# Block combination and transposition moved by one step, and the first gates made on TensorE, in a state-space and expert-mixture kernel

## The chip, the cores and the metric

The kernel runs on one core of a Trainium2 chip. The metric is the device time of one execution in microseconds (us); the median of several executions is compared. A core has these engines, each with its own queue of instructions that runs in order: PE (TensorE, matrix products into PSUM), DVE (VectorE), ACT (ScalarE), POOL (GpSimd) and SP (SyncE, which here issues most transfers). Everything is in float32.

## The reference

A Mamba-2 state-space block (4 sequences, 8 heads, 768 positions, head width 32, state 16) feeds a merge of four expert networks. Cut to what matters:

```python
# block 1, by chunks of the sequence, state carried along
cum = np.cumsum(log_a[chunk]);  L = exp(cum_i - cum_j) * causal
y = (C @ B.T * L) @ x + (C @ state) * exp(cum)
state = exp(cum_last) * state + sum_j B_j x_j exp(cum_last - cum_j)
# block 2, on rows of 256 = 8 heads * 32
p = domain_probs / (domain_probs.sum(-1, keepdims=True) + 1e-09)
for e in range(4):
    h = np.maximum(x @ w1[e], 0.0)            # 256 -> 1024
    out += p[:, e:e + 1] * (h @ w2[e])        # 1024 -> 256
```

## The kernel before, in words

**Tiling.** The sequences are cut into 24 chunks of 128 tokens. A block is four chunks, the same place of all four sequences: 512 tokens, and there are six blocks (k = 0 to 5). For every block the expert part takes eight steps (r = 0 to 7; an expert e is two steps, each with half of its hidden width), 48 steps in all (n = 8k + r). The state-space part of the next block's chunks is woven into the steps of the current block: chunk c comes in (`masks`, `decay_part`, `scores`, `masked`) in steps r = 0, 2, 4, 6, and goes out (`outputs`, later `carry`) in steps r = 1, 3, 5, 7. In the last block no chunk comes in.

**A step.** From step 2 on both layers are done by a fast scheme of seven products for a 2x2 split of the matrices instead of eight. `fmul(n, i)` is product i of the first layer (L436, four pieces on PE, into the PSUM banks X and Y); `snap` copies X on ACT (L443); `total` adds Y and a copy to z on DVE (L448); `gated` applies the ReLU and the gate on DVE (L458); `diff` makes the differences T1 to T4 that the second layer needs (L465, DVE). `smul(n - 1, i)` is product i of the second layer of the step before (L521), into four PSUM accumulators `acc0` to `acc3`, each held for a whole block. The first two steps use the eight plain products (`plain_first` L485, `plain_second` L502). `sum_w1` and `sum_w2` make sums of weights on POOL (L160 to L164) in the first block and store them in DRAM for the later ones (`w1_d`, `w2_d`).

**Order.** The schedule is written out by hand: every engine runs its instructions in the order of the program text, and the framework adds the waits. A tile with a tag shares a fixed number of buffers; taking one anew waits for all readers of the old one. Two waits of this kind matter here: a new product into Y waits for the `total` that read it, and the first `smul` of a block into an accumulator waits for the readers of the block before. Transfers use eight counters in turn, so that a transfer also waits for the eighth before it.

**The end of a block.** In step r = 0 of block k the last products of block k - 1 are made. `keep` copies `acc0` and `acc1` to SBUF (ACT). `combine(k - 1, 0)` adds on DVE into u (L541), `combine(k - 1, 1)` makes four adds on POOL (L544 to L547), both at the end of step r = 0. `combine(k - 1, 2)`, two adds on DVE from `acc2` and `acc3` (L549, L550; a third, L552, in the first block), is in the list `late`, which runs in step r = 1 behind `gated(n, "11")`, after the differences T2 and T4. Then `turned_out` transposes 32x32 squares on DVE (L610), and `leave` sends the rows to the output with eight transfers on SP's queue (L618), one quarter of the block in each of the steps r = 1 to 4.

**The first gates.** The normalized probabilities `pr` are transposed by PE (L266), copied by ACT to `p_sb`, 96 rows of 128 (L268), and stored by ACT's queue in DRAM as `p_d` (L269). `load_gate(k, e)` then reads the rows of a block and an expert and spreads each over all 128 partitions (L273, SP's queue, 256 KB). Before step 2, the front of the program, the order on DVE is: `masked(2)` (L363), `decays(3)` (L330, two scans), `plain_gated(0, 1)` (two `gated`, the first readers of a gate), `masked(3)`, `plain_gated(1, 1)`; on PE: `outputs(1)` (L382), `scores(2)` (L353), `plain_first(0, 1)`, `outputs(2)`, `scores(3)`, `plain_first(1, 1)`, `outputs(3)`, `plain_second(0, 1, ...)`. `outputs(c)` waits for `masked(c)`.

Of the kernel before, what the change touches and what calls it, by code (L numbers as in the profile page):

```python
# [17 lines left out]
def kernel(  # L18
# [90 lines left out]
    def load_decays(c, queue):  # L109
        if c >= SPREAD:  # L110
            ab = load.tile([P, NH * P], FP32, tag="ab", name="ab")
            nc.sync.dma_start(
                out=ab, in_=acut_d[real(c)].rearrange(
                    "h s -> (h s)").partition_broadcast(P))
            st.setdefault(c, {})["ab"] = ab
        if c >= CPB:
            ah = st[c]["ah"] = load.tile([HN, P], FP32, tag="ah", name="ah")
            queue.dma_start(out=ah, in_=ac_d[real(c)].unsqueeze(1).to_broadcast([NH, N, P]))
# [19 lines left out]
    def load_w2(n):  # L138
        e, jj = divmod(n % SPB, JJ)
        t2 = wt2[n] = wts.tile([P, 7 * HB], FP32, tag="wt2", name="wt2", bufs=5)  # L140
        if n >= SPB:
            nc.sync.dma_start(out=t2, in_=w2_d[n % SPB])
            return
        for i in range(2):
            f = i * FH + jj * HB
            nc.sync.dma_start(
                out=t2[:, i * 2 * HB:(i + 1) * 2 * HB].rearrange("p (j m) -> p j m", j=JJ),
                in_=w2[e, f:f + HB].rearrange("(j p) m -> p j m", p=P))
# [113 lines left out]
    def turn_gates():  # L262

        rows = T // P * E
        pp = ps_att.tile([rows, P], FP32, tag="att", name="pp")
        nc.tensor.transpose(pp, pr.rearrange("p i e -> p (i e)"), ident[:, 0])  # L266
        p_sb = const.tile([rows, P], FP32, name="p_sb")
        nc.scalar.copy(out=p_sb, in_=pp)  # L268
        nc.scalar.dma_start(out=p_d.rearrange("i e s -> (i e) s"), in_=p_sb)  # L269

    def load_gate(k, e):
        g = gate[k, e] = ffn.tile([P, CPB, P], FP32, tag="gate", name="gate", bufs=3)
        nc.sync.dma_start(out=g, in_=p_d.rearrange(  # L273
            "(i k) e s -> k e i s", k=NBLK)[k, e].partition_broadcast(P))
# [71 lines left out]
    def scores(c, homes):  # L346

        s = st[c]
        s["g"] = []
        for q, (pool, tag) in enumerate(homes):  # L350
            k = slice(32 * q, 32 * q + 32)
            g = pool.tile([P, NT, P], FP32, tag=tag, name="g")
            nc.tensor.matmul(  # L353
                out=g.rearrange("p t s -> p (t s)"), lhsT=s["xb"][k, OBT:OBT + P],
                rhs=s["ctm"][k].rearrange("p t s -> p (t s)"),
                start=True, stop=True, tile_position=(32 * q, 0))
            s["g"].append(g)
# [9 lines left out]
    def outputs(c, pool, tag):  # L367

        s = st[c]
        k, i = divmod(c, CPB)  # L370
        first = k == 0
        w = P + N if k < NBLK - 1 else P
        xb, MT = s["xb"], s["MT"]
        y = pool.tile([P, NT, P + N], FP32, tag=tag, name="y")
        if not first:
            nc.tensor.matmul(  # L376
                out=y[:, :, 0:P], lhsT=state[i][1].rearrange("p q d -> p (q d)"),
                rhs=s["cts"], start=True, stop=False, skip_group_check=True)
        for t in range(NT):
            for q in range(NQ):  # L380
                h = NQ * t + q
                nc.tensor.matmul(  # L382
                    out=y[32 * q:32 * q + 32, t, 0:w], lhsT=xb[:, h * D:h * D + D],
                    rhs=MT[:, NT * q + t, 0:w], start=(first and t == 0), stop=True,
                    tile_position=(0, 32 * q), skip_group_check=True)
        if i == 0:
            yT[k] = ffn.tile([P, NT, BLK], FP32, tag="yT", name="yT")
        nc.scalar.copy(out=yT[k][:, :, i * P:i * P + P], in_=y[:, :, 0:P])
        if w > P:
            s["A"] = att.tile([P, NT, N], FP32, tag="A", name="A", bufs=4)  # L390
            nc.scalar.copy(out=s["A"], in_=y[:, :, P:])
# [83 lines left out]
    def plain_first(n, b, a=(0, 1)):  # L475

        k = n // SPB
        cols = slice(b * HB - HB, b * HB)
        f = first.setdefault(n, {})
        for bank, ws in [(("X", (A11, A12)), ("Y", (S3, A22)))[i] for i in a]:  # L480
            pool, tag = (ps_f, bank) if n or b > 1 else (ps_s, {"X": "acc2", "Y": "acc3"}[bank])
            f[bank] = pool.tile([P, JJ, HB], FP32, tag=tag, name=bank)
            for j in range(JJ):
                for i, w in enumerate(ws):
                    nc.tensor.matmul(  # L485
                        out=f[bank][:, j], lhsT=wt1[n][:, w, j * P:j * P + P],
                        rhs=yT[k][:, i, cols], start=(i == 0 and j == 0), stop=(i == 1),
                        skip_group_check=True)
# [171 lines left out]
    sum_w1(0, 0)  # L660
    masked(1, range(NQ))
    outputs(1, ps_att, "att")
    load_decays(3, nc.sync)
    load_w2(1)
    load_w1(2)
    load_w2(2)

    scores(2, homes)
    plain_first(0, 1)
    decays(2)  # L670
    sum_w1(1, 0)
    masks(3)
    load_gate(0, 0)
    load_chunk(4)
    load_gate(0, 1)
    load_w1(3)
    load_w2(3)
    masked(2, range(NQ))
    outputs(2, ps_att, "att")

# [3 lines left out]
    load_w1(4)  # L684
    load_w2(4)
    sum_w2(0, 0)
    plain_gated(0, 1)
    plain_first(1, 1)
    masked(3, range(NQ))
    sum_w2(1, 0)  # L690
# [28 lines left out]
    for n in range(PLAIN, NS):  # L719
        k, r = divmod(n, SPB)  # L720

        enter, exit = ({2: 1, 4: 2, 6: 3}, {2: 0, 3: 1, 5: 2, 7: 3}) if k == 0 else (
            {0: 0, 2: 1, 4: 2, 6: 3}, {1: 0, 3: 1, 5: 2, 7: 3})
        c_in, c_out = (CPB * (k + 1) + d[r] if r in d and k < NBLK - 1 else None
                       for d in (enter, exit))
        ending = r == 0 and k > 0
        e = r // JJ
        if r % JJ == 0 and n + JJ < NS:
            load_gate(*divmod(n // JJ + 1, E))
        if PLAIN + 2 < n + 2 < NS:  # L730
            load_w1(n + 2)
            load_w2(n + 2)
        opened(n)
        total(n, 1, "11")
        gated(n, "11", "z11")
        for work in late:
            work()
        if c_in is not None:
            masks(c_in)
            decay_part(c_in, 0)  # L740
        if n == PLAIN:
            for m in range(PLAIN):
                sum_w1(m, 1)
        elif n == PLAIN + 1:
            for m in range(1, PLAIN):
                sum_w2(m, 1)
        sum_w1(n + 2)
        if n > PLAIN:
            sum_w2(n + 1)
        if r == 1 and k > 0:  # L750
            turned_out(k - 1)
        if k > 0 and 1 <= r <= CPB:
            leave(k - 1, r - 1)
        smul(n - 1, 1)
        fmul(n, 6)
        snap(n, 6)
        smul(n - 1, 3)
        if ending:
            keep(k - 1, 0)
        if c_out is not None:  # L760
            outputs(c_out, ps_att, "att")
        fmul(n, 5)
        fmul(n, 7)
        snap(n, 7)
        total(n, 7, "22")
        smul(n - 1, 7)
        smul(n - 1, 5)
        if ending:
            keep(k - 1, 1)
        gated(n, "22", "z22")  # L770
        if c_in is not None:
            decay_part(c_in, 1)
        if n == PLAIN:
            sum_w2(0, 1)
        if c_out is not None and c_out + 2 < NCH:
            load_chunk(c_out + 2)
        fmul(n, 3)
        total(n, 6, "12")
        fmul(n, 4)
        gated(n, "21", "X")  # L780
        gated(n, "12", "z12")
        if r == SPB - 1 and k < NBLK - 1:
            sums(k + 1)
        smul(n - 1, 6)
        smul(n - 1, 2)
        if c_in is not None:
            scores(c_in, ((ps_att, "att"), (ps_att, "att"), (ps_f, "X"), (ps_f, "Y")))
            masked(c_in, (2, 3, 0, 1))
        diff(n, "T3", "22", "12")
        if c_in is not None:  # L790
            decay_part(c_in, 2)
        if ending:
            combine(k - 1, 0)
            combine(k - 1, 1)
        smul(n - 1, 4)
        diff(n, "T1", "12", "11")
        late = [lambda n=n: diff(n, "T2", "22", "T1"), lambda n=n: diff(n, "T4", "21", "T2")]
        if ending:
            late.append(lambda k=k: combine(k - 1, 2))
        if PLAIN < n <= CPB:  # L800
            late.append(lambda n=n: carry(n - 1))
        if c_out is not None:
            late.append(lambda c=c_out: carry(c))
# [48 lines left out]
```

## Time and profile before

| | |
|---|---|
| median of 8 runs | 662.6 us (660.0 to 663.84) |
| the profiled execution | 663.84 us; its span, first to last instruction, 662.1 us |
| mean granted clock of PE | 0.993 |
| busy share | PE 98%, DVE 74%, ACT 17%, POOL 17% |
| mean DMA rate | 192 GB/s, 127.09 MB in all |

The page gives busy times by engine, then the span in 40 slices of 16.55 us, in which a digit is a tenth of a slice, then groups of instructions by source line. `L448` is line 448 of the kernel. The list of waits has lines "who waited <- for whom: us in total, times, longest". Lines of the timeline have start and duration in us, engine (PEld is PE's loading of weights), line, operation, the tile written <- the tiles read, the shape, the number of instructions merged, and in brackets the idle time before and what ended it. A float32 product appears as two pieces on PE. The ends of pieces on PE are modelled, so lost time is read from start to start.

### The profile page before, as it was taken

The numbers are of one execution on the slowest core, as the hardware profiler recorded it, in microseconds if no ns is written. First come the engines' busy times: TensorE is split into PE (matmuls) and PEld (weight loads), VectorE is DVE, ScalarE is ACT, GpSimd is POOL, SyncE is SP. The second block draws the span as 40 slices with busy tenths as digits, with TensorE's granted clock in tenths as the row PEclk, the third lists the DMA queues.
The fourth block names the chain that finished last, engine by engine and source line by source line (L and its number), as shares of the span: only waits on it lengthen the run. The fifth ranks groups of instructions, "written<-read, shape, count | busy, mean of one in ns | idle before, by whom it ended". The sixth has DMA issues, their size and how long they took to land. (4 is left out here: it accounts for less than half of the span.)

```text
span 662.1 us, 8901 instructions
## 1 busy us (share of the span) xinstructions
PE 647.6 (98%) x3359; PEld 542.1 (82%) x3359; DVE 488.7 (74%) x814; ACT 115.1 (17%) x246; POOL 112.4 (17%) x157
## 2 busy tenths in 40 slices
PE   7899989999999999999999999999999999999997
PEld 4688868888888888888887888888888888888886
DVE  8667878798686788866879768668867686766655
ACT  3011111221112121121122111212111112111110
POOL 5757494020000002000003000000200000100000
PEclk9899989999999999999999999999999999999999
DMA  7989998404668611678630656941276751176000
GB/s 234 312 309 338 335 365 311 171 35 114 236 209 354 238 56 26 228 254 304 253 146 1 182 193 240 356 181 56 71 248 210 291 219 59 18 245 243 4 1 32
DMA packets 68666, 127.09 MB, mean 192 GB/s; under 512 B 26616, under 2 KB 50576, under 8 KB 68624
## 3 DMA queue, kind: packets, MB, share of 16 engines
q1 hardware_dynamic: 65568, 111.32, 48.7%
q0 software_dynamic: 2304, 14.68, 5.5%
q10 hardware_dynamic: 752, 0.54, 0.3%
q8 instruction: 26, 0.43, 0.2%
q14 instruction: 16, 0.13, 0.1%
HBM read 108.44 MB, written 18.07 MB: 191 GB/s over the span
## 5 line engine op out<-in xcount | busy, mean ns | idle before, releaser
L448 DVE TENSOR_TENSOR z<-Y,snap 128x512 f32<-128x512 f32 x138 | 94.5, 685 | 125.1 <-ACT snap L443 71.5
L521 PE MATMUL acc<-hT,wt 128*128 128x256 f32 x736 | 183.1, 382 | 0.0
L443 ACT COPY snap<-X 128x512 f32<-128x512 f32 x138 | 80.9, 587 | 472.5 <-PE X L436 472.5
L521 PEld LDWEIGHTS acc<-hT,wt 128*128 128x128 f32 x736 | 138.3, 190 | 24.0 <-issue 6.0
L436 PE MATMUL X<-yS,wt 128*128 128x256 f32 x552 | 141.7, 379 | 0.0
L521 PE MATMUL acc<-h,wt 128*128 128x256 f32 x552 | 141.5, 379 | 0.0
L436 PEld LDWEIGHTS X<-yS,wt 128*128 128x128 f32 x552 | 105.0, 190 | 14.4
L521 PEld LDWEIGHTS acc<-h,wt 128*128 128x128 f32 x552 | 104.9, 190 | 14.3
L458 DVE SCALAR_TENSOR_TENSOR h<-z,gate 128x512 f32<-128x512 f32 x138 | 98.7, 715 | 3.5 <-PE acc L502 0.4
L436 PE MATMUL Y<-yT,wt 128*128 128x256 f32 x368 | 94.9, 380 | 2.4 <-DVE z L448 2.4
L436 PEld LDWEIGHTS Y<-yT,wt 128*128 128x128 f32 x368 | 68.4, 189 | 14.5 <-DVE z L448 4.3
L465 DVE TENSOR_TENSOR hT<-h,hT 128x512 f32<-128x512 f32 x92 | 69.8, 759 | 1.6
L465 DVE TENSOR_TENSOR hT<-h,h 128x512 f32<-128x512 f32 x92 | 64.6, 726 | 0.8
L330 DVE TENSOR_TENSOR_SCAN LT<-ab,ident 128x512 f32<-128x512 f32 x42 | 53.5, 1276 | 0.9 <-DMA ab<-acut_d 0.9
L335 POOL TENSOR_TENSOR MT<-xb,LT 128x128 f32<-128x128 f32 x20 | 8.8, 438 | 252.0 <-PE Y L436 132.5
L436 PE MATMUL Y<-yS,wt 128*128 128x256 f32 x184 | 50.2, 396 | 0.0
L436 PE MATMUL X<-yT,wt 128*128 128x256 f32 x184 | 47.2, 379 | 0.0
L363 DVE TENSOR_TENSOR MT<-g,LT 128x256 f32<-128x256 f32 x96 | 33.9, 416 | 17.3 <-PE g L353 17.3
L316 POOL TENSOR_TENSOR cts<-ctm,dec 128x256 f32<-128x256 f32 x20 | 18.5, 927 | 160.6 <-ACT snap L443 157.7
L458 DVE SCALAR_TENSOR_TENSOR h<-X,gate 128x512 f32<-128x512 f32 x50 | 34.3, 686 | 12.1 <-PE X L436 4.6
L436 PEld LDWEIGHTS Y<-yS,wt 128*128 128x128 f32 x184 | 33.8, 192 | 8.5 <-issue 4.2
L436 PEld LDWEIGHTS X<-yT,wt 128*128 128x128 f32 x184 | 35.0, 190 | 4.8
(91 smaller groups left out, 339.2 us busy)
## 6 DMA issues: line engine op xcount, KB each, us to landing
wt<-w_d SPq DMA_DIRECT2D x80, 896.0 KB, 10.0
w_d<-wt POOLq DMA_DIRECT2D x16, 896.0 KB, 6.8
ab<-acut_d SPq DMA_DIRECT2D x21, 512.0 KB, 4.7
wt<-in_w_dram SPq DMA_DIRECT2D x32, 256.0 KB, 7.4
xb<-in_xbc_dram SPq DMA_DIRECT2D x24, 320.0 KB, 3.8
gate<-p_d SPq DMA_DIRECT2D x24, 256.0 KB, 8.7
out_dram<-ot SPq DMA_DIRECT2D x160, 16.0 KB, 5.2
ah<-ac_d SPq DMA_DIRECT2D x20, 64.0 KB
```

Source lines behind the costliest of these rows:

```text
L316: nc.gpsimd.tensor_mul(cts, s["ctm"], dec.unsqueeze(1).to_broadcast([HN, NT, P]))
L330: nc.vector.tensor_tensor_scan(out=LT[:, i * w:i * w + w], data0=s["a"][i], data1=ident.rearrange("p h s -> p (h s)")[:, :w], initial=0.0, ...
L335: nc.gpsimd.tensor_mul(s["MT"][:, :, P:], s["xb"][:, OB:OB + HN].rearrange("p (h n) -> p h n", h=NH), s["LT"][:, :, P - 1:P].to_broadcast( ...
L363: nc.vector.tensor_mul(s["MT"][:, h, 0:P], s["g"][q], s["LT"][:, h])
L436: nc.tensor.matmul(out=f[bank][:, j], lhsT=wt1[n][:, w, j * P:j * P + P], rhs=rhs, start=(i in (1, 2, 5) and j == 0), stop=(j == JJ - 1), ...
L443: nc.scalar.copy(out=s, in_=first[n]["X"])
L448: nc.vector.tensor_add(z, first[n]["Y"], first[n][i])
L458: nc.vector.scalar_tensor_tensor(out=h, in0=first[n][src], scalar=0.0, in1=g.unsqueeze(1).to_broadcast([P, JJ, HB]), op0=ALU.max, op1=ALU. ...
L465: nc.vector.tensor_sub(h[o], h[x], h[y])
L521: nc.tensor.matmul(out=acc[k, u][:, half], lhsT=w2_op(n, w)[:, j], rhs=rhs[:, j], start=(begins and j == 0), stop=(n % SPB == SPB - 1 and ...
```

## The change

There are three edits. First, `p_d` is stored by SP's queue instead of ACT's, and the gates of block 0 and expert 0 are no longer loaded: `spread_gate`, behind `outputs(1)`, multiplies a spread column of the identity with `p_sb` on PE, once for each of the four chunks, into one PSUM tile, which ACT copies to the gate's tile. Second, the order in the front is changed: the first half of `plain_first(0, 1)` (X) stands ahead of `scores(2)`, and `gated(0, "11")` stands ahead of `masked(2)` on DVE. Third, at a block's end `combine` 0 and 1 move from the end of step r = 0 to step r = 1 behind the late work, `combine` 2 moves behind `gated(n, "22")` of step r = 1, `turned_out` moves to the end of step r = 1, and `leave` takes the steps r = 2 to 5.

```diff
         p_sb = const.tile([rows, P], FP32, name="p_sb")
+        gate["rows"] = p_sb
         nc.scalar.copy(out=p_sb, in_=pp)
-        nc.scalar.dma_start(out=p_d.rearrange("i e s -> (i e) s"), in_=p_sb)
+        nc.sync.dma_start(out=p_d.rearrange("i e s -> (i e) s"), in_=p_sb)
+
+    def spread_gate():
+
+        p_sb = gate["rows"]
+        g = ps_att.tile([P, CPB, P], FP32, tag="att", name="gp")
+        for i in range(CPB):
+            r = real(i) * E
+            nc.tensor.matmul(
+                out=g[:, i], lhsT=ident[:T // P * E, 0, r:r + 1].to_broadcast([T // P * E, P]),
+                rhs=p_sb, start=(i == 0), stop=True, skip_group_check=True)
+        gate[0, 0] = ffn.tile([P, CPB, P], FP32, tag="gate", name="gate", bufs=3)
+        nc.scalar.copy(out=gate[0, 0], in_=g)
...
     outputs(1, ps_att, "att")
+    spread_gate()
     load_decays(3, nc.sync)
...
+    plain_first(0, 1, (0,))
     scores(2, homes)
-    plain_first(0, 1)
+    plain_first(0, 1, (1,))
     decays(2)
     sum_w1(1, 0)
     masks(3)
-    load_gate(0, 0)
     load_chunk(4)
     load_gate(0, 1)
     load_w1(3)
     load_w2(3)
+    gated(0, "11", "X")
     masked(2, range(NQ))
     outputs(2, ps_att, "att")
...
-    plain_gated(0, 1)
+    gated(0, "21", "Y")
     plain_first(1, 1)
...
         for work in late:
             work()
+        if r == 1 and k > 0:
+            combine(k - 1, 0)
+            combine(k - 1, 1)
...
-        if r == 1 and k > 0:
-            turned_out(k - 1)
-        if k > 0 and 1 <= r <= CPB:
-            leave(k - 1, r - 1)
+        if k > 0 and 2 <= r < CPB + 2:
+            leave(k - 1, r - 2)
...
         gated(n, "22", "z22")
+        if r == 1 and k > 0:
+            combine(k - 1, 2)
...
-        if ending:
-            combine(k - 1, 0)
-            combine(k - 1, 1)
         smul(n - 1, 4)
         diff(n, "T1", "12", "11")
+        if r == 1 and k > 0:
+            turned_out(k - 1)
...
-        if ending:
-            late.append(lambda k=k: combine(k - 1, 2))
```

## The prediction

> **What bounds the kernel now.** I read the page first: which engine has no idle time.
>
> ```profile
> PE 647.6 (98%) x3359; PEld 542.1 (82%) x3359; DVE 488.7 (74%) x814; ACT 115.1 (17%) x246; POOL 112.4 (17%) x157
> ...
> PEclk9899989999999999999999999999999999999999
> ```
>
> TensorE (PE) is busy 98% of 662.1 us, so an edit is worth what it takes from PE's few holes; VectorE (DVE) at 74% counts only where PE waits for it. The clock row has two dents near the start. Next the list of waits, for the holes.
>
> ```profile
> DVE h L458 <- DMA gate<-p_d: 4.1, 1, 4.1
> ...
> PE Y L436 <- DVE z L448: 2.4, 4, 0.8
> ...
> PE y L376 <- POOL cts L316: 2.3, 1, 2.3
> ...
> PE y L382 <- DVE MT L363: 1.9, 1, 1.9
> ```
>
> Of PE's waits the first belongs to the front: DVE waits 4.1 us for the first gates, and behind that PE waits 1.9 us for `masked(3)`. The four waits for z come once at each of the first four block changes. The one for `cts` is near 90 us. The list gives total, times and longest, in us. Then the timeline around 25 us (start, duration; DVE, then PE) and the stretches around it (PE busy, ..., granted clock, DMA share).
>
> ```profile
> 15.45 1.39 DVE L363 TENSOR_TENSOR MT<-g,LT 128x256 f32<-128x256 f32 x4
> 17.77 2.74 DVE L330 TENSOR_TENSOR_SCAN LT<-ab,ident 128x512 f32<-128x512 f32 x2 [0.93 <-DMA ab<-acut_d]
> 24.61 0.69 DVE L458 SCALAR_TENSOR_TENSOR h<-X,gate 128x512 f32<-128x512 f32 x1 [4.09 <-DMA gate<-p_d]
> ```
>
> ```profile
> 23.21 1.89 PE L485 MATMUL Y<-yT,wt 128*128 128x256 f32 x8
> 27.03 0.92 PE L382 MATMUL y<-MT,xb 128*32 128x144 f32 x16 [1.94 <-DVE MT L363]
> 27.88 5.41 PE L502 MATMUL acc<-h,wt 128*128 128x256 f32 x16
> ```
>
> ```profile
> 25.00:28.40 3.40, 1.46 (x19) 1.04 (x19) 3.40 (x9) 0.41 (x3) 3.24 (x5) 1.00 0.78 219
> 28.40:31.90 3.50, 3.50 (x10) 2.73 (x9) 3.22 (x5) 0.64 (x3) 3.02 (x5) 0.51 1.08 380
> ```
>
> Eight pieces take 1.73 us start to start (two rows L485 of this kind follow each other at that pitch), so y(3) was due at 23.21 + 1.73 = 24.94 and starts at 27.03: 2.1 us lost. Its 16 followers need 5.24 us to the next group (33.12) where 3.5 would do: the granted clock is 0.51 in the stretch behind the hole, another 1.7. Last, one block change (PE, then DVE).
>
> ```profile
> 467.97 1.89 PE L521 MATMUL acc<-hT,wt 128*128 128x256 f32 x8
> 470.42 1.13 PE L436 MATMUL Y<-yT,wt 128*128 128x256 f32 x4 [0.56 <-DVE z L448]
> ```
>
> ```profile
> 468.55 1.25 DVE L610 STREAM_TRANSPOSE ot<-o 128x1024 f32<-128x1024 f32 x1
> 469.71 0.65 DVE L448 TENSOR_TENSOR z<-Y,snap 128x512 f32<-128x512 f32 x1
> ...
> 476.84 0.69 DVE L448 TENSOR_TENSOR z<-Y,snap 128x512 f32<-128x512 f32 x1 [1.77 <-PE Y L436]
> ```
>
> Due at 467.97 + 1.73 = 469.70, started at 470.42: 0.72 lost, because the transposition stands ahead of `total(n, 7)`; 1.77 us of idle DVE lie at the step's end. The same sum gives 0.99, 0.67 and 0.67 at the changes near 152, 258 and 364 us, and nothing at the fifth, where no chunk enters: 3.05 us in all (the 2.4 in the list of waits leaves out the refill of PE's pipeline).
>
> **The front, part by part.** Times are of the profiled execution.
>
> Store of `p_d` to SP's queue. `p_sb` is ready at 10.60. On ACT the issue stood until 13.30 and held `masks(2)` to 13.75, hence both `yT` copies. SP has nothing to issue between 9.4 and 12.9, where it waits for `acut_d`; 0.40 of issue hides there. If the store waits on SP as it did on ACT, `ab(3)` and the weights behind it slip 0.75: `ab(3)` lands at 18.4, still before DVE wants it (below). Cost nothing; without that cover 0.4 to 0.75.
>
> `load_gate(0, 0)` goes: 256 KB, and SP's wait from 16.7 to 17.84 for the store's landing. What is queued behind (`load_chunk(4)`, gate (0, 1), `load_w1(3)`...) moves up 1 to 2 us.
>
> `spread_gate`: four products of 128 columns, two pieces each. No row shows this form. At the end transposes of 128x128 follow each other at 0.11 us, which gives 0.9; the broadcast weights of L296 with 256 columns go at 0.216, which gives 1.7. The width is that of the first, so 0.9 plus 0.1 for the first load: 1.0. ACT's copy of 128x512 is a `snap`: 0.59, beside PE.
>
> PE's new order: y(1) ends at 14.3; `spread_gate` to 15.3; X (its `yT` copy is ready at about 14.8, with ACT free) to 17.0; scores to 17.8, at 0.7 as in the earlier rows of L353, because the PSUM buffers for which they took 1.40 at 14.49 are free by then; Y to 19.6; y(2) at 19.7, where it was 19.48. So PE is 0.2 late (0.1 to 1.0 by the two prices).
>
> DVE now waits with `gated(0, "11")` for X until 17.3; queued behind are `masked(2)` and `decays(3)`, and PE's y(2) waits for the former. 0.65 + 1.39 ends at 19.4: in time. `decays(3)` 2.4 to 2.7 (to 22.0), `gated(0, "21")` to 22.7, `masked(3)` to 24.1. PE is through `plain_first(1, 1)` at 25.1: no hole, hence no slow stretch. POOL's MT(3) waits for these scans and comes 1.3 us later; its chain of sums then ends at about 35.1, and the next thing it waits for (MT(4), now 38.74) comes at 35.1 too. Gain 2.1 + 1.7 - 0.2 = 3.6.
>
> Here the Trainium skill speaks against the second term: "TensorE: Matmul & The Clock Gate", section "Why this matters for your kernels", asks only that idle gaps stay under about 3 us. By it the slow stretch would not belong to a gap of 1.94, and the front would gain 1.9. The trace shows 0.51 right behind this gap and again behind the only other one as long, so the measurement decides.
>
> What is late next: PE's wait for `cts(6)` at 90.6. POOL stands there behind sums that waited 8.88 us for weights, landed at 80.7. That load goes back over SP and the stores of sums to POOL's MT(4), which follows PE, so it moves along; but the DMA share is 1.0 from 28 to 42 and at most about 0.65 from 42 to 50, so some of it may not. With 3.6 us less in which some 3 to 4 us of the engines are idle before 80, I take 0.4 given back (0 to all 3.6). Net 3.2.
>
> **The block changes.** In step r = 1 (times of the change at 462; PE's due times without the stall): DVE has T1 462.2, z11, `gated` 11, T2 and T4 at pitches of 0.6 to 0.7, since POOL's adds no longer run beside them (beside them T1 took 1.21 and T2 with T4 2.35): free at 465.4. The add into u, 0.40, starts POOL's four adds at 465.9; at 0.73 to 1.18 each they end between 468.8 and 470.6. z22 waits for its `snap` alone (468.17 + 0.59 = 468.76), ends at 469.5, and PE's Y starts when due. `gated` 22 to 470.1; the two adds from PSUM to 470.9 (a third in the first block, 0.34). PE's next start in `acc2` is due at 469.70 + 2 x 0.865 = 471.43: 0.5 to spare; with `gated` 22 at 1.2 beside POOL nothing to spare, and up to 0.35 lost in the first block. z12, two `gated`, T3 and T1 to 474.2, transposition to 475.4; the next z is due at 476.1. Gain 3.05 (2.0 to 3.05).
>
> The skill's page "SBUF — State Buffer", section "Who interferes with whom", says that a VectorE instruction with two SBUF inputs and a GpSimd one that reads SBUF exclude each other for a whole instruction. By it `gated` 22 could wait for a whole add, 1.18 by the row above instead of 0.5, and 0.7 be lost at each change.
>
> `leave` moves one step back: eight issues, 3.7 us of SP. At r = 2 that step's weights stand ahead of it; behind it are the next step's, wanted two steps (some 26 us) later and landing in 10. Cost nothing.
>
> **Sum.** 663.84 - 3.2 - 3.05 = 657.6 against the profiled execution (span 662.05, 1.8 around it). The median is 1.24 lower: 656.4.
>
> **Rivals.**
> 1. The front's gain is eaten at 90 us: weights land when they did, PE comes 3.6 earlier and waits 5.9 instead of 2.3. For it: the DMA share of 1.0; against it: the dips from 42 to 50, at 62 and 74. 662.6 - 3.05 = 659.5; 661.2 if a second slow stretch of 1.7 follows. Chance 0.18.
> 2. Stalls at the changes only move: POOL's adds collide with `gated` 22 and the adds, and `acc2` is 0.6 late at each. 656.4 + 3.0 = 659.4. Chance 0.07.
> 3. Slower: `acc2` is given back so late that PE idles there. Before, its readers ran ahead of z22; now they stand in a queue behind z22, `gated` 22 and POOL. It decides from 471.43 on: front and changes together hold 6.2 us, so over 1.5 us late at each of five changes the kernel is slower by over 1.3. At 1.94, the shortest hole with a slow stretch behind it, it costs 5 x (1.94 + 1.7) = 18: 674.5. Against it: the sum ends 0.5 early, and POOL has nothing else in that step. Chance 0.09.
> 4. The first gates do not set the front (weights do), or the new order waits as long: 662. Against it: sums and weights of these steps are done by 26. Chance 0.04.
>
> **Numbers.** The sum has 0.62. A run tells about 0.2% (1.3 us) from no change. Faster: 0.62, most of 1 (0.15) and of 2 (0.05): 0.82. Same: 0.03 + 0.01 + 0.04 = 0.08. Slower: 0.09 + 0.01 = 0.10. The range goes down to nothing given back (0.4), the slow stretch at 93 us gone by chance of its position (1.7) and 1.1 of the runs' spread, and up over rival 1 to part of its slow stretch: 653.2 to 660.8.
>
> **What would show it.** Right: no DVE wait for a gate's DMA; no PE wait for MT near 25 us, one dent in the clock instead of two; y(3) near 25.1; the PE wait for `cts` at 2.3 to 2.8, some 3.5 us earlier; PE Y without a wait for z. Wrong: PE acc L521 waiting for L549 or L550, a wait for `cts` near 6, or DVE idle over 2 us before `gated(0, "11")`.

## The result and the profile after

The change takes 657.6 us (median of 20 runs, 656.07 to 659.2) against 662.25 us (57 runs): ratio 0.9937, 95% interval 0.9925 to 0.9949, so 3.4 to 5.0 us faster. The forecast was a gain of 6.25 us, to 656.4 us, in the range 653.2 to 660.8. The profiled execution took 657.99 us, with a span of 656.2 us. The change adds 13 lines ahead of most of the code: L436 is now L449, L448 is L461, L521 is L534.

First the page after: engines, and the granted clock of PE in 40 slices.

```profile
PE 647.5 (99%) x3367; PEld 543.2 (83%) x3367; DVE 484.0 (74%) x814; ACT 115.9 (18%) x247; POOL 111.4 (17%) x157
...
PEclk9999989999999999999999999999999999999999
...
L449 PE MATMUL Y<-yT,wt 128*128 128x256 f32 x368 | 94.5, 379 | 0.0
```

One dent is left of two, and the products into Y have no idle time before them. PE's waits after (total, times, longest):

```profile
PE y L389 <- POOL cts L329: 2.7, 1, 2.7
```

PE's waits for MT and for z at the block changes are gone, and so is DVE's wait for the gate's transfer; PE's wait for `cts` has grown from 2.3 to 2.7. The front on the timeline after, DVE and then PE:

```profile
17.97 0.69 DVE L471 SCALAR_TENSOR_TENSOR h<-X,gate 128x512 f32<-128x512 f32 x1 [1.91 <-PE X L498]
18.58 1.41 DVE L376 TENSOR_TENSOR MT<-g,LT 128x256 f32<-128x256 f32 x4
20.08 2.34 DVE L343 TENSOR_TENSOR_SCAN LT<-ab,ident 128x512 f32<-128x512 f32 x2
22.33 0.67 DVE L471 SCALAR_TENSOR_TENSOR h<-Y,gate 128x512 f32<-128x512 f32 x1
22.91 1.41 DVE L376 TENSOR_TENSOR MT<-g,LT 128x256 f32<-128x256 f32 x4
```

```profile
14.34 0.70 PE L395 MATMUL y<-MT,xb 128*32 128x144 f32 x16
14.97 1.16 PE L278 MATMUL gp<-p_sb,ident 96*128 96x128 f32 x8
15.96 1.89 PE L498 MATMUL X<-yT,wt 128*128 128x256 f32 x8
17.79 0.71 PE L366 MATMUL g<-ctm,xb 32*128 32x256 f32 x8
...
20.36 0.70 PE L395 MATMUL y<-MT,xb 128*32 128x144 f32 x16
...
25.91 0.70 PE L395 MATMUL y<-MT,xb 128*32 128x144 f32 x16
26.53 3.72 PE L515 MATMUL acc<-h,wt 128*128 128x256 f32 x16
```

The second row of MT is `masked(3)`: it ends at 24.3, before PE wants y(3) at 25.91, so there is no hole, and the 16 pieces behind it go at full clock (3.72 us instead of 5.41). The next group starts at 30.09, before at 33.12. PE reached y(1) 0.72 later than in the profiled execution of before (14.34 against 13.62). The record of the granted clock begins, at full, at 10.1 us here and at 4.6 there, and ahead of that the same eight pieces into g took 1.34 us here (at 6.50) and 0.71 there (at 6.33): PE was at half clock for longer. A block change after, PE and then DVE:

```profile
462.99 1.89 PE L534 MATMUL acc<-hT,wt 128*128 128x256 f32 x8
464.72 1.03 PE L449 MATMUL Y<-yT,wt 128*128 128x256 f32 x4
```

```profile
460.43 0.42 DVE L554 TENSOR_TENSOR u<-acc,kept 128x256 f32<-128x256 f32 x1
463.81 0.69 DVE L461 TENSOR_TENSOR z<-Y,snap 128x512 f32<-128x512 f32 x1 [2.97 <-ACT snap L456]
...
469.18 1.24 DVE L623 STREAM_TRANSPOSE ot<-o 128x1024 f32<-128x1024 f32 x1
```

Y starts 1.73 us behind the row before it, when it is due. The add into u is done long before, z waits for its `snap` alone, 2.97 us, and the transposition lies in DVE's idle time at the step's end.

### The profile page after: what moved, and what is told of

It is laid out like the page before. It is cut to its first block, busy times and chain, and to the rows that moved or that the text cites. A ratio compares the mean times of both kernels' runs of the same rounds, so it can differ in the third digit from the quotient of the medians.

```text
span 656.2 us, 8922 instructions
## 1 busy us (share of the span) xinstructions
PE 647.5 (99%) x3367; PEld 543.2 (83%) x3367; DVE 484.0 (74%) x814; ACT 115.9 (18%) x247; POOL 111.4 (17%) x157
## 4 chain that ended last, share of the span: by engine, by line
PE 95%; POOL 1%; DMA 1%; DVE 0%; issue 0%; SPq 0%; ACT 0%; POOLq 0%
PE acc L534 41%; PE X L449 24%; PE Y L449 18%; PE g L366 3%; PE y L395 2%; PE acc L515 2%; PE y L389 1%; DMA wt<-in_w_dram 1%; PE X L498 1%; PE Y L498 1%; PE a L309 1%; PE t L651 1%; POOL wt L164 0%; POOL wt L161 0%; POOL wt L162 0%
## 5 line engine op out<-in xcount | busy, mean ns | idle before, releaser
L461 DVE TENSOR_TENSOR z<-Y,snap 128x512 f32<-128x512 f32 x138 | 94.6, 686 | 129.2 <-ACT snap L456 84.6
L534 PE MATMUL acc<-hT,wt 128*128 128x256 f32 x736 | 183.3, 382 | 0.0
L534 PEld LDWEIGHTS acc<-hT,wt 128*128 128x128 f32 x736 | 138.6, 190 | 24.2 <-issue 6.0
L449 PE MATMUL X<-yS,wt 128*128 128x256 f32 x552 | 142.5, 381 | 0.0
L534 PE MATMUL acc<-h,wt 128*128 128x256 f32 x552 | 141.5, 379 | 0.0
L449 PEld LDWEIGHTS X<-yS,wt 128*128 128x128 f32 x552 | 105.5, 191 | 14.5
L534 PEld LDWEIGHTS acc<-h,wt 128*128 128x128 f32 x552 | 104.9, 190 | 14.3
L449 PE MATMUL Y<-yT,wt 128*128 128x256 f32 x368 | 94.5, 379 | 0.0
L449 PEld LDWEIGHTS Y<-yT,wt 128*128 128x128 f32 x368 | 68.7, 190 | 10.8 <-DVE z L461 0.2
L478 DVE TENSOR_TENSOR hT<-h,hT 128x512 f32<-128x512 f32 x92 | 66.4, 722 | 1.6
L449 PE MATMUL Y<-yS,wt 128*128 128x256 f32 x184 | 50.0, 395 | 0.0
L449 PE MATMUL X<-yT,wt 128*128 128x256 f32 x184 | 47.2, 379 | 0.0
L449 PEld LDWEIGHTS Y<-yS,wt 128*128 128x128 f32 x184 | 33.6, 191 | 8.2 <-issue 4.4
L449 PEld LDWEIGHTS X<-yT,wt 128*128 128x128 f32 x184 | 35.0, 190 | 4.8
```

Source lines behind the costliest of these rows:

```text
L449: nc.tensor.matmul(out=f[bank][:, j], lhsT=wt1[n][:, w, j * P:j * P + P], rhs=rhs, start=(i in (1, 2, 5) and j == 0), stop=(j == JJ - 1), ...
L461: nc.vector.tensor_add(z, first[n]["Y"], first[n][i])
L478: nc.vector.tensor_sub(h[o], h[x], h[y])
L534: nc.tensor.matmul(out=acc[k, u][:, half], lhsT=w2_op(n, w)[:, j], rhs=rhs[:, j], start=(begins and j == 0), stop=(n % SPB == SPB - 1 and ...
```

## The experiments

All kernels are timed against before on the same chip. A stretch, below, is 3.41 us in which the granted clock is at half.

| | runs | median, us | ratio to before, 95% interval |
|---|---|---|---|
| e1, block changes alone | 12 | 660.05 | 0.9955 (0.9934 to 0.9976) |
| e2, front alone | 12 | 661.12 | 0.9982 (0.9966 to 0.9999) |
| e3, transposition alone | 8 | 658.95 | 0.9946 (0.9925 to 0.9967) |
| e4, `cts(6)` first | 4 | 654.76 | 0.9888 (0.9865 to 0.9910) |
| e5, store on SP alone | 10 | 662.09 | 0.9996 (0.9976 to 1.0015) |
| e6, `spread_gate`, old order | 10 | 661.61 | 0.9976 (0.9957 to 0.9996) |
| e7, new order alone | 4 | 668.83 | 1.0089 (1.0063 to 1.0114) |
| e8, e4 with `sum_w2(7)` later | 4 | 653.28 | 0.9854 (0.9834 to 0.9875) |
| e9, e8 with the old front | 6 | 655.29 | 0.9895 (0.9865 to 0.9926) |
| e10, e8 with the old order | 6 | 653.76 | 0.9876 (0.9848 to 0.9903) |
| e11, the change again | 12 | 657.34 | 0.9930 (0.9908 to 0.9952) |

**e1 and e2: which half is short?** e1 has the loop of after and the front of before; e2 the reverse.

```diff
 # e1: before, and of the change only
+        if r == 1 and k > 0:
+            combine(k - 1, 0)
...
 # e2: before, and of the change only
+    spread_gate()
+    plain_first(0, 1, (0,))
...
```

> Front as before; combine, turned_out and leave as after. Theory (the sum holds, and only the half-clock term was too large for the median): 3.05 us faster than before, ratio 0.9954, since this part has no clock term; no PE wait for z in its profile, the hole of about 2 us at 25 us still there. Rival (the shortfall of the median lies in the block changes: losses there are smaller in undisturbed runs, or return elsewhere): 1.5 us faster or less, ratio above 0.9977.

> Front as after; block changes as before. Theory: in the profile no hole at 25 us, a PE wait for cts of 2.3 to 2.8 us, and 0.7 to 1.0 us lost at four block changes as before; in the median 1.2 to 2.0 us faster (2.1 of the hole, less 0.2 and 0.4, and the half-clock stretch of 1.7 counted only for the part of the runs of before that have it). Rival (the front is worth its full 3.2 in the median too): ratio 0.9952 or less.

e1 gains 0.0045 of 662 us, 3.0 us, where the sum had 3.05, and its list of waits has none for z. e2 gains 1.2 us, and the most that its interval allows (0.0034 of 662, 2.3 us) excludes the forecast's 3.2. Together they make the 4.2 us of the change, so the shortfall is the front's. In e2's list of waits:

```profile
PE y L389 <- POOL cts L329: 3.3, 1, 3.3
...
PE Y L449 <- DVE z L461: 2.4, 4, 0.8
```

The four waits for z are those of before; the wait for `cts` is 1.0 longer than before. e1's profile still has the hole of the front, and there it is 3.44 us long, not 1.94.

**e3: is the transposition the whole stall?** `turned_out` moves, and with it `leave` by one step (left out below); `combine` stays where it was.

```diff
-        if r == 1 and k > 0:
-            turned_out(k - 1)
...
         diff(n, "T1", "12", "11")
+        if r == 1 and k > 0:
+            turned_out(k - 1)
```

> Before, with only turned_out moved to the end of step r = 1 and leave one step back; combine stays where it was, its POOL adds beside T1, gated 11, T2 and T4. Theory (the transposition ahead of z22 is the whole stall): DVE is through combine 2 at the time at which z22's snap is done, so all but 0 to 0.3 us (first block) of the 3.05 us is gained: 2.7 to 3.05 us faster, ratio 0.9954 to 0.9959. Rival (POOL's adds that slow DVE share the cause): half of it, 1.5 us, remains lost, ratio about 0.9977, and PE still waits for z.

In e3's profile PE loses nothing at any change, and the ratio is not above e1's. T2 and T4 still run beside POOL's adds, but there is time to spare (e3, DVE):

```profile
461.31 2.35 DVE L465 TENSOR_TENSOR hT<-h,hT 128x512 f32<-128x512 f32 x2
...
464.67 0.69 DVE L448 TENSOR_TENSOR z<-Y,snap 128x512 f32<-128x512 f32 x1 [0.34 <-ACT snap L443]
```

T2 and T4 take 2.35 us as before (1.41 in the change, where POOL has no adds beside them), yet DVE idles 0.34 us before z. Moving the combination was not needed.

**e5, e6, e7: what made the front's hole.** Each adds one part of the front to before.

```diff
 # e5
-        nc.scalar.dma_start(out=p_d...
+        nc.sync.dma_start(out=p_d...
 # e6: e5, and
+    spread_gate()
-    load_gate(0, 0)
 # e7: before, and
+    plain_first(0, 1, (0,))
     scores(2, homes)
+    plain_first(0, 1, (1,))
...
+    gated(0, "11", "X")
     masked(2, range(NQ))
...
+    gated(0, "21", "Y")
```

> Before, with only the store of p_d moved from ACT's queue to SP's; the gate of block 0 is still loaded. Theory (the gate's arrival sets the hole at 25 us): the store lands by 14.5, SP issues the gate's load at about 16.7 instead of 17.9, it lands 1.2 us earlier, and the hole shrinks from about 2.1 to 0.9 us; a hole of 0.9 leaves the clock at 1.00; 1.2 to 2.9 us faster by where the run had a half-clock stretch. Rival (the load is bound by the DMA engines, whose share is 1.0 there): it lands when it did, the hole and the time stay.

> Before, with the store on SP and spread_gate in place of load_gate(0, 0), but X, scores(2), masked(2) and plain_gated(0, 1) in the old order. Theory (the gate's transfer alone made the hole; the new order is not needed): both gated calls run near 21, masked(3) ends near 23, no PE hole at 25 us; the front's gain is all here, time as e2 (ratio 0.997 to 0.9985). Rival (the order holds a part): a PE hole of 0.5 us or more stays in the front, 0.5 to 1 us slower than e2.

> Before, with only the new order (X ahead of scores(2), gated 11 ahead of masked(2), gated 21 ahead of masked(3)); the gate of block 0 is still loaded, its store on ACT. Theory (gated 11 holds DVE until the gate lands at 24, and masked(2) with PE's y(2) behind it): PE idles about 6.5 us ahead of y(2), near 19.7 to 26.3, then one or two half-clock stretches; y(3) comes near 32 instead of 27; 4 to 7 us slower, ratio 1.006 to 1.010. Rival (PE's later waits for weights and cts take it up): less than 1.5 us slower, ratio below 1.002.

e5 came out as its rival said. SP issued the gate's load at 16.99 instead of 17.89, but it landed at 24.54, after 7.5 us, where before had it at 24.10, after 6.2. The DMA share was 1.03 from 17 to 20 us, 1.01 to 22 and 0.95 to 24.5: in this profile the earlier issue brought no earlier landing.

e6 came out as the theory said, with no wait of PE in the front: the two `gated` start at 20.76 and 21.34, `masked(3)` at 22.15. But the old order costs PE something there (e6, PE):

```profile
15.77 1.44 PE L366 MATMUL g<-ctm,xb 32*128 32x256 f32 x8
...
20.79 0.70 PE L395 MATMUL y<-MT,xb 128*32 128x144 f32 x16
```

Its `scores(2)` take 1.44 us, in the change 0.71. From y(1) to y(2) PE needs 6.7 us in the profiles of e6 and e10 (old order) and 6.0 in those of the change, e2, e4, e8 and e11 (new order).

e7 came out as the theory said too, 5.9 us slower. DVE stands before the gate with `masked(2)` queued behind it, and PE with it (e7, DVE and then PE):

```profile
24.00 0.69 DVE L458 SCALAR_TENSOR_TENSOR h<-X,gate 128x512 f32<-128x512 f32 x1 [7.82 <-DMA gate<-p_d]
```

```profile
25.84 1.41 PE L382 MATMUL y<-MT,xb 128*32 128x144 f32 x16 [5.81 <-DVE MT L363]
```

So taking the gate off the transfers is the edit that closes the hole. The new order does not close it; with the gate off the transfers it saves 0.7 us of PE in the profiles, and without that it does harm.

**e4 and e8: the wait that is left.** In step 4 POOL sums late weights ahead of MT(6) and `cts(6)`, for which PE waits.

```diff
-        if n > PLAIN:
+        if n > PLAIN and n != CPB:            # e8: n not in (CPB, SPB - 2)
             sum_w2(n + 1)
+        if n == SPB - 1:                      # e8 only
+            sum_w2(n)
...
             decay_part(c_in, 2)
+        if n == CPB:
+            sum_w2(n + 1)
```

> After, with one more move: in step 4 sum_w2(5) stands on POOL behind decay_part(6, 2) instead of ahead of it. Theory (PE's wait of 2.7 us for cts(6) comes from POOL's order, and the half-clock stretch behind it from that wait): cts(6) is done near 86, before y(6) is due at 87.6; no PE wait for cts, no 0.5 clock behind it; 2.7 + 1.7 = 4.4 us faster than the change, some 8.6 us faster than before, ratio 0.987. Rival (cts waits for DVE's dec or for the late weights anyway): the wait stays above 1.5 us and the ratio at 0.992 to 0.994.

> e4 with one more move: sum_w2(7) stands on POOL in step 7 instead of step 6. Theory (the 1.6 us that PE lost in e4 at 103.8 come from POOL's sums beside DVE's differences and carry, which put z22 late): no PE wait above 0.3 us between 12 us and the end; 1.6 us faster than e4, 653.2 us, ratio 0.9862 to 0.987. Rival (DVE is late there by its own work): the wait stays above 1 us and the time at 654.7.

e4 has no wait for `cts` and no half clock there. By the ratios it is 3.2 us faster than the change, not the 4.4 expected: near 104 us there is a new hole, where DVE's differences run beside POOL's sums and take 2.85 us instead of 1.41 (e4, the wait, then DVE):

```profile
PE Y L449 <- DVE z L461: 1.4, 1, 1.4
```

```profile
99.55 2.85 DVE L478 TENSOR_TENSOR hT<-h,hT 128x512 f32<-128x512 f32 x2
```

e8 takes that away too: no wait of PE above 0.2 us between 12 us and the end, PE 99% busy, a span of 651.2. Its ratio is 0.0083 below the change's, 5.5 us of 662 (the medians, measured at different times, differ by 4.3), and its four runs lie within 0.8 us (652.98 to 653.78), where the 57 of before spread over 5.5. It is faster than both kernels.

**e9, e10, e11: what the front is worth alone.** e9 is e8 with the front of before, so that the hole at 25 us is the only one; e10 is e8 with e6's front; e11 is the change as it is.

```diff
 # e9, against e8
-    spread_gate()
+    load_gate(0, 0)
 # e10, against e8
-    plain_first(0, 1, (0,))
     scores(2, homes)
-    plain_first(0, 1, (1,))
+    plain_first(0, 1)
...
```

> e8 with the front of before (gate loaded, old order): the only hole left is that at 25 us. Theory (the half-clock stretch behind that hole comes in a part of the runs only, so the prediction's 1.7 us was counted in full where a third of it was due): runs fall into two groups by granted clock, about a third at 0.997 or 0.998 and the rest at 0.999 to 1.000; the median is 1.5 to 2.5 us above e8, 654.8 to 655.8. Rival (each such hole halves the clock, as the two profiled ones did): all runs at 0.997 or 0.998 and the median 3.3 to 3.8 above e8, 656.6 to 657.1.

> e8 with spread_gate but the old order of X, scores(2), masked(2) and plain_gated(0, 1). Theory (as e6: the gate's transfer alone made the hole): no PE wait in the front, within 0.4 us of e8 (its PE order makes scores(2) wait 0.7 us for PSUM, which e8 avoids, so if anything 0.3 to 0.7 slower). Rival (the order is worth a part of the front): 1 us or more slower than e8.

> The change itself on the same chip as the two above, for its granted clocks by run. Theory: 657.6 us, ratio to before 0.9925 to 0.995; no run at a clock under 0.995 (one hole left, that for cts), while a third of the runs of before are (two holes). Rival: runs at 0.993 to 0.995 as in before.

The median of e9 is 2.0 us above that of e8, measured at another time, and 1.5 above that of e10, measured beside it, as the theory said and not the 3.3 to 3.8 of the rival. The mean clocks do not fall into the two groups expected: all six are between 0.998 and 1.000, and the profiled run, at 0.998, has no stretch before its end. So in e9 the hole costs its idle time alone. It is there in the profile, and the clock behind it is full (e9, two windows of 3.4 us; PE busy first, granted clock 1.00 in the third column from the end):

```profile
23.23:26.64 3.41, 2.18 (x11) 1.57 (x9) 1.45 (x3) 0.00 (x0) 3.25 (x5) 1.00 0.87 276
26.64:30.05 3.41, 2.43 (x23) 1.98 (x24) 3.38 (x9) 1.05 (x4) 2.95 (x5) 1.00 0.96 263
```

e10 has no wait of PE in the front, and its median is 0.5 above that of e8, measured at another time; the 0.7 us by which its `scores(2)` take longer would do it. The ratios put 1.5 us between the two, with intervals that overlap, so its rival (1 us or more) is not excluded by the times. e11 agrees with the result. The expectation that no run would be under 0.995 failed by one run of 12, at 0.993; the others are at 0.996 or more.

**The clocks of all runs together.** One stretch takes 0.0026 off the mean clock of 660 us, and the half clock at a run's very end, which all profiles but e8's have within the span, takes less than 0.002. So a mean granted clock up to 0.995 means two stretches, 0.996 to 0.997 one, 0.998 and more none. The mean clock is known for 61 runs of before and 33 of the change:

| runs by stretches | two | one | none | mean number |
|---|---|---|---|---|
| before | 16, median 664.3 us | 23, 662.8 us | 22, 661.2 us | 0.90 |
| the change | 1 (662.5 us) | 26, 657.6 us | 6, 656.5 us | 0.85 |

One stretch costs some 1.1 to 1.6 us by these medians (the single run with two, 4.9 above the others, lost something else besides), and the change has on average nearly as many of them as before.

## Why the prediction was right, and what was mis-sized

**Right: sign, range, mechanism.** The forecast case came about. The rivals (gain eaten at 90 us, stalls moved, `acc2` late) did not: the profile shows no hole of their kind.

**`spread_gate` and the order.** 1.0 us was worked out from the transposes' pitch; the row takes 15.96 - 14.97 = 0.99. PE was to be 0.2 late at y(2): 20.36 less the 0.72 of the later start is 19.64, 0.16 behind the old 19.48. The store cost nothing, as said (e5). Not seen was that the hole closes with the old order too (e6); the new order is worth 0.7 us of PE in the profiles, which is not clear of the noise in the times.

**The block changes.** Times less the shift of 4.98 us (PE's due time 469.70 against 464.72): the add into u due at 465.4 came at 465.41, z22 due at 468.76 came at 468.79, the transposition due at 474.2 came at 474.16. POOL's four adds took 0.72 or 0.73 each with DVE idle beside them, the low end. The gain of 3.05 was 3.0 in e1, and e3 shows that the transposition alone is its cause. The Trainium skill's rule on two SBUF inputs ("SBUF — State Buffer", "Who interferes with whom") put 0.7 at risk at each change; `gated` 22 and the adds did not overlap, so no run of the change tests it there.

**The give-back: the size was right in part by luck.** 0.4 was taken, and the wait for `cts` grew from 2.33 to 2.67 in the profile of after, by 0.34, though to 3.3 in e2. But the load of weights before it did not move along with PE: it landed at 79.68 instead of 80.74, 1.1 earlier, while PE came to `cts` 2.8 earlier. Most of the rest was made up by POOL, which went from its first sum to `cts` in 9.85 us instead of 11.23. The DMA share of before, too, was 0.71 from 44 to 46 us, not at most about 0.65.

**The step that failed in size is the clock term.** "Another 1.7" was put in full because one profiled execution of before had the stretch. From one profiled execution to the other the sum is nearly right: 657.6 forecast, 657.99 measured. The error lies on the way to the median. The profiled execution of before was the highest of its eight times, with a mean clock of 0.993, so one with two stretches; of the 61 runs only 16 had two. One stretch is 1.1 to 1.6 us by the table, so much of the 1.24 us by which the median of before was lower is that second stretch. To take off 1.24 from the forecast as well counts it twice: the change's profiled execution has one stretch, as most of its runs do, and lies only 0.4 above their median. With 0.90 against 0.85 stretches the term is 0.05 x 1.7, about 0.1 us. The sum is then 2.1 - 0.2 - 0.4 + 0.1 = 1.6 for the front (e2: 1.2) and with 3.05 a total of 4.65: the medians differ by 4.65, the ratio gives 4.2.

The stretch of the removed hole was thus given back in another way than rival 1 had it: 27 of the change's 33 runs have at least one, and without the wait for `cts` none of the 14 runs of e4, e8 and e10 has one, so it is that hole, a little longer, that has a stretch behind it. In before at most 39 of the 61 runs can have had one there. Why it became more frequent is not shown.

**The hole itself** is no constant either: in the five profiles with the old front and order its idle time is 1.94, 3.44, 1.18, 1.68 and 2.21 us (before, e1, e3, e5, e9). It ends when the gate's load lands (at 24.10, 26.07, 24.20, 24.54 and 24.68; DVE's first `gated` starts 0.5 us behind it in each), and PE comes to it earlier or later as the clock comes up at the start (4.6 to 11.0 us). From y(1) to y(3) these five take 12.35 to 15.03 us, 13.44 on average, and the five with the front of the change 11.56 or 11.57. That is 1.9 us, what the sum had as 2.1 - 0.2; that its one profile, with 13.41, lay near the average was luck. Before absorbed a late start in the hole (1.18 and 1.68 are the profiles with the clock up at 11.0 and 10.6); the change, with no hole, does not. That this costs the median something is argued, not shown.

## What to carry to other kernels

A hole is worth its idle time, which itself differs from run to run, and its half-clock stretch only by a chance that one profile cannot give: read the granted clock of many runs before the stretch goes into a sum, and ask whether the profiled run is a typical one before its distance to the median is carried over. When a hole that waits for a transfer is closed, follow the same queue to the next wait; here moving two of POOL's sums there (e8) was worth as much as the whole change. A long in-order instruction belongs behind the last short one that another engine waits for: moving the transposition, with the output behind it, brought all of the 3 us.

## What the runs showed of the hardware

In all 13 profiles the granted clock changes at multiples of 3.413 us from its first entry, and a halving goes with little work of PE inside one such window, not with the length of a gap. Three profiles show the window that holds the hole (PE busy is the first figure behind the length); the clock was halved behind the first, and not behind the other two. After:

```profile
88.63:92.04 3.41, 1.57 (x19) 1.00 (x20) 3.34 (x5) 0.18 (x1) 3.31 (x5) 1.00 1.02 425
```

e1, its wait for `cts` of 2.5 us, and the window behind it:

```profile
90.92:94.33 3.41, 1.61 (x8) 1.07 (x6) 3.34 (x5) 0.59 (x1) 3.09 (x5) 1.00 0.94 386
94.33:97.75 3.42, 2.73 (x25) 2.02 (x26) 2.57 (x3) 0.46 (x2) 3.26 (x5) 1.00 1.00 414
```

e5, the hole of 1.68 us in the front:

```profile
24.26:27.67 3.41, 1.73 (x14) 1.21 (x12) 2.59 (x7) 0.00 (x0) 3.10 (x6) 1.00 0.98 284
```

In e9, above, a hole of 2.21 us falls into two windows (2.18 and 2.43 busy), and neither is followed by half clock, while before's hole of 1.94 us, inside one window, is. Ten windows at full clock in the profiles of before, after, e1, e2, e3, e5, e6, e7 and e11, with 0 to 1.57 us of PE work, were followed by half clock, and six in e1, e3, e4, e5 and e9, with 1.61 to 2.43, were not. Two do not fit: one in e7 with 1.42 kept the full clock, and the last of e9 with 1.61 was followed by half. So the limit lies near 1.4 to 1.7 of 3.41 us, 40 to 50%, and the same hole is dear or cheap by where the grid falls. What decides inside that band stays open, as does why e7's clock stayed at half for three windows (1.02, 3.41 and 3.41 us of PE work), where the others had one. The page "TensorE: Matmul & The Clock Gate" of the Trainium skill, section "What's actually happening", states the length of the window, which these records confirm, and asks for an idle one; here a window almost half busy was enough.
